# Attention scores on row-tiled halves of TensorE replaced by block-diagonal matmuls on the whole array

## The chip, the core and the metric

The kernel runs on one core of a Trainium2 chip. Its engines work in parallel, each through its own queue in order: TensorE (PE in the profile, with its weight loads as PEld), VectorE (DVE), ScalarE (ACT), GpSimd (POOL) and SyncE (SP, which here only issues DMAs). The metric is the device time of one execution in microseconds (us), the median of several runs.

## What is computed

Two stages. The first is attention within blocks whose keys and values are a soft permutation of blocks. For each of 4 batches and 8 heads, with 768 rows of 64 in 8 blocks of 96:

```
P = sort_net                                   # [4, 8, 8, 8]
5 times: P = exp(P - max); P /= row sums; P /= column sums
k_sorted = einsum('bhij,bhjcd->bhicd', P, k_b) # blocks of k mixed by P
v_sorted = einsum('bhij,bhjcd->bhicd', P, v_b)
scores   = q_b @ k_sorted^T / 8                # per block, 96 x 96
out      = softmax(scores) @ v_sorted
```

The second is a feed-forward network (FFN) on the 3072 x 512 result: `h = relu(x @ w_in)`, `out = (h * h) @ w_out`, with a hidden size of 2048.

## The kernel before

**Plan.** Every operation is put down with an engine, a cost and what it depends on; a list scheduler (`Plan.run`) works out an order, and the instructions are emitted in that order on every engine. For TensorE there are two queues, each in order: attention and FFN. An FFN "chunk" is the four up matmuls of one hidden tile or a quarter of one output tile's down matmuls; 28 chunks make a unit of 384 tokens, and there are 8 units. An attention stage's head goes ahead of the next FFN chunk once its due time, counted in chunks, is reached and its inputs are ready. `DUES` (lines 21 to 49) holds these due times by batch and stage: K (sort the second half of batch 0), S (scores), T (turn the values), A (scores times values), X (turn the result), V and N (sort values and keys in natural layout), Z (DMA transposes), Q (batch 1's first two pairs), L (loads). Attention stages are queued by due time, and stages whose due time is negative go as soon as they can. Batch 0's first half is in an order written out by hand (`FIRST`, line 53); FFN begins behind it at about 21.6 us.

**Tiles.** A `Unit` is a pair of heads (hp) of one batch. Both heads' q^T lie above each other on 128 partitions: head 0 on 0 to 63, head 1 on 64 to 127. Scores are computed in halves, that is in groups of four blocks (`s_sc`, line 641), into one of two PSUM slots (ring `r2`).

- The *row form* (line 665) is used for all of batch 0 and for the first two pairs of batch 1. Each block and head has a matmul of its own with 64 contraction rows and 96 columns: 8 per group, two of them on different row halves of the array at a time. The plan gives it 0.17 us and the mode "row"; each change of mode costs 0.1 us in the plan. Its q^T is in the `qT` tiles, written by `s_q` (line 523).
- The *wide form* (line 655) is used for the pairs from batch 1's third on (`u.tiled`). A buffer qz holds q^T block-diagonally, that is head 0 over zeros and zeros over head 1, side by side. One matmul with 128 contraction rows and 192 columns then does both heads of a block: 4 per group. The block-diagonal form is made by `q_split` (line 840): VectorE copies head 1's half to its place and zeroes where it was. GpSimd zeroes head 0's other half once (`make_zeros`, line 804), after batch 0, since the qz buffers are batch 0's value buffers (vs) until then.

ScalarE takes exp of a group (lines 685, 695, 701), TensorE multiplies by the values (line 871), VectorE normalises (lines 883 and 884), and the result is turned into xT, the FFN's input, by TensorE and a copy or by a DMA.

**Loads.** All inputs come by GpSimd DMAs, in order: batch 0, w_in, w_out, then batch 1's six loads (`loads_after`, line 379); later batches are loaded when the batch before them is done. xT (128 x 4 x 3072) is filled batch by batch; a region of it, that of the last batch, holds the selection matrix `sel` in the beginning (line 391).

Of the kernel before, what the change touches and what calls it, by code (L numbers as in the profile page):

```python
# [10 lines left out]
AF = mybir.ActivationFunctionType  # L11
# [9 lines left out]
DUES = {  # L21
    (0, "K"): (-130.0, -51.0, -121.0, -51.0),
    (0, "S"): (-63.0, -37.0, -72.5, -31.0),
    (0, "T"): (-110.5, -2.0, -40.5, -38.0),
    (0, "A"): (-47.0, 2.0, -9.5, -15.5),
    (0, "X"): (-8.5, 4.5, 11.0, -2.5),
    (0, "W"): (-102.5,),
    (1, "V"): (4.5, 5.0),
    (1, "Q"): (21.0,),
    (1, "N"): (None, 39.0),  # L30
    (1, "Z"): (None, None, 42.0, 44.5),
    (1, "S"): (26.0, 36.5, 43.0, 47.0),
    (1, "A"): (39.5, 41.0, 44.0, 48.5),
    (1, "X"): (41.0, 41.0, 49.0, 48.5),
    (2, "L"): (49.5,),
    (2, "N"): (57.0, 78.0),
    (2, "V"): (63.5, 89.0),
    (2, "Z"): (68.5, 90.0, 94.0, 91.0),
    (2, "S"): (90.5, 96.5, 99.5, 98.5),
    (2, "A"): (95.5, 96.5, 104.0, 103.5),  # L40
    (2, "X"): (96.5, 99.0, 118.5, 114.5),
    (3, "L"): (124.0,),
    (3, "N"): (138.5, 138.0),
    (3, "V"): (136.0, 143.0),
    (3, "Z"): (144.0, 146.5, 159.5, 156.0),
    (3, "S"): (151.5, 154.0, 160.0, 158.0),
    (3, "A"): (152.0, 156.0, 162.5, 158.0),
    (3, "X"): (162.0, 257.5, 169.0, 366.0),
}
# [135 lines left out]
def kernel(  # L185
# [10 lines left out]
    nc = tc.nc  # L196

    B, H, S, D = q.shape
# [5 lines left out]
    HP = H // 2  # L204
# [105 lines left out]
    w_out_bf = const.tile([128, NT, d_model], BF16)  # L310
    xT = const.tile([128, KC, n_tok], BF16)
    w_all = const.tile([128, H + HP, NB, C0], BF16)
    w_t = const.tile([128, NH // 4, 4, NB], BF16)
# [65 lines left out]
    def loads_after(deps):  # L379
        for g in range(4):  # L380
            if g == 1:
                landed["last"] = plan.add("DMA", 0.4, lambda e: None, [landed["last"]])
            t = slice(NT // 4 * g, NT // 4 * (g + 1))
            dma(("w_out", g), 1.05, lambda t=t: (w_out_bf[:, t, :], w_out_r[:, t, :]), deps)
        for t, g in ((2, 0), (2, 1), (1, 0), (0, 0), (1, 1), (0, 1)):
            load(1, t, HP * g, HP, deps=deps)

    rs = const.tile([NH, NB], FP32)
    cs = const.tile([NH, NB], FP32)
    pf = const.tile([NH, NB, NB], BF16)  # L390
    sel = xT[0:32, 0, 3 * S:3 * S + 32 * C0].rearrange("p (j c) -> p j c", c=C0)
    pt = const.tile([128, NB, NH], BF16)
# [112 lines left out]
    class Unit:  # L505


        def __init__(self, b, hp, halves):
            self.b, self.hp, self.halves = b, hp, halves
            self.tiled = in_tiles(b, 1, HP * (hp // 2))  # L510
            if self.tiled:
                self.i0, self.ni, self.full = 0, NB, True
                return
            self.n, self.old = rks.take()
            self.kvT = kvT_r[self.n]
            self.ksT, self.vsT = self.kvT[:, 0, :], self.kvT[:, 1, :]
            self.i0, self.ni = NQ * halves[0], NQ * len(halves)
            self.full = len(halves) == 2
# [4 lines left out]
    def s_q(b, hp, p0, p1, due=0, after=None, eng=AD):  # L523

        n = p1 - p0
        t = {}

        def mm(e):
            qb = qkv[b][0]
            if b == 0:  # L530
                t["p"] = psf.tile([128, NA, n], BF16, tag="pf", name="qtp")
            else:
                t["p"] = ps1.tile([128, NA, n], BF16, tag="p1", name="qtp")
            for a in range(NA):
                for h in range(2):
                    nc.tensor.transpose(
                        out=t["p"][64 * h:64 * (h + 1), a, :],
                        in_=qb[p0:p1, 2 * hp + h, D * a:D * (a + 1)],
                        identity=ident[p0:p1, p0:p1])
            if p0 == 0:  # L540
                tiles["qT", b, hp] = att.tile(
                    [128, NA, 128], BF16, tag="qT", name="qT", bufs=4)

        def ev(e):
            qT, src = tiles["qT", b, hp].rearrange("p a x -> p (a x)"), t["p"]
            if b == 0:
                copy(e, qT.rearrange("p (i c a) -> p i c a", a=NA, c=C0)
                     [:, p0 // C0:p1 // C0, :, :], src.rearrange("p a (i c) -> p i c a", c=C0))
            else:
                copy(e, qT.rearrange("p (i a c) -> p i a c", a=NA, c=C0)  # L550
                     [:, p0 // C0:p1 // C0, :, :], src.rearrange("p a (i c) -> p i a c", c=C0))

        if b == 0:
            dep = landed[b, 0, 0, p0]
        else:
            dep = landed[b, 0, HP * (2 * hp // HP), 0]
        ring = rf if b == 0 else r1
        s1, old = ring.take()
        if p0 == 0:
            qTs[b, hp], oldq = rqT.take()  # L560
        else:
            oldq = []
        pe = plan.add("PE", 0.04 + 0.0023 * n, mm, [dep, id_op] + old, due, mode="col")
        readers[b].append(pe)
        op = one_of(eng, cost_b(NA * n), ev, [pe, after] + oldq)
        ring.use(s1, pe, op)
        rqT.use(qTs[b, hp], op)
        return op
# [72 lines left out]
    def s_sc(u, due=0):  # L641
# [3 lines left out]
        for hf in u.halves:  # L645
# [4 lines left out]
            def mm(e, hf=hf, st=st, slot=slot):  # L650
                st["p"] = scp = p2[slot]
                if u.tiled:
                    for n in range(NQ):
                        i = NQ * hf + n
                        nc.tensor.matmul(  # L655
                            out=scp[:, n // 2, 2 * BLK * (n % 2):2 * BLK * (n % 2 + 1)],
                            lhsT=kx_r[u.kx][:, i::NB],
                            rhs=qz_r[u.qz][:, :, :, C0 * i:C0 * (i + 1)],
                            start=True, stop=True)
                    return  # L660
# [11 lines left out]
            u.et[hf], olde = ret.take()  # L672
            if u.tiled:
                pe = plan.add("PE", 0.33, mm, [u.k_op, u.q_op] + old, due)
                rkx.use(u.kx, pe)
                rqz.use(u.qz, pe)
            else:
# [5 lines left out]
            if u.b == 0:  # L683
                def ex(e, st=st, et=et_r[u.et[hf]]):
                    nc.scalar.activation(out=et[:, :, 0:HS], in_=st["p"][0:96, :, 0:HS],  # L685
                                         func=AF.Exp, scale=scale)

# [4 lines left out]
            for h in range(2):  # L692
                def ex(e, h=h, st=st, et=et_r[u.et[hf]]):
                    if u.tiled:
                        nc.scalar.activation(  # L695
# [4 lines left out]
                        return  # L700
                    nc.scalar.activation(
                        out=et[:, h, 0:HS].rearrange("p (n c a) -> p n c a", c=C0, a=NA),
                        in_=st["p"][0:96, h, 0:HS].rearrange("p (n a c) -> p n c a", c=C0, a=NA),
                        func=AF.Exp, scale=scale)
                op = plan.add("ACT", cost_f(HS)[0], ex, [pe] + olde)
# [98 lines left out]
    def make_zeros(e):  # L804
        for qz in qz_r:
            nc.gpsimd.memset(qz[0:64, 1, :, :], 0.0)

    def s_turn(b, hp):

# [29 lines left out]

        def q_split(e):  # L840
            nc.vector.tensor_copy(out=qz[64:128, 1, :, :], in_=qz[64:128, 0, :, :])
            nc.vector.memset(qz[64:128, 0, :, :], 0.0)

        sp = plan.add("SP", 1.4, q_turn, [qp, loaded(b)] + oldz + [op for ops in rvs.all for op in ops])
        q_op = plan.add("WAY", 1.3, lambda e: None, [sp])
        rqi.use(n, q_op)
        if not zeroed:
            last = [op for ops in rvs.all for op in ops if op.eng0 == "PE"]
            assert len(last) == 2 * HP
            zeroed.append(plan.add("POOL", 2.1, make_zeros, last))  # L850
        q_op = plan.add("DVE", 0.8, q_split, [q_op, zeroed[0]])
        rqz.use(z, q_op)
        return kx, z, k_op, q_op

    def s_av(u, due=0):
# [4 lines left out]
        for hf in u.halves:  # L860
# [4 lines left out]
            def mm(e, hf=hf, st=st, slot=slot):  # L865
# [3 lines left out]
                for n in range(NQ):  # L869
                    for h in range(2):  # L870
                        nc.tensor.matmul(  # L871
                            out=oup[:, h, 66 * n:66 * n + D + 1],
                            lhsT=(et_r[u.et[hf]].rearrange("p h x -> p (h x)")
                                  [:, BLK * (2 * n + h):BLK * (2 * n + h) + 128] if u.tiled else
                                  et_r[u.et[hf]][:, h, BLK * n:BLK * n + 128]),
# [187 lines left out]
    for hp in range(HP):  # L1063
        qops[hp] = s_q(0, hp, 0, 64, after=exps[2 + (hp + 2) // 3], eng="ACT")
    q2ops = [s_q(0, hp, 64, 128, after=exps[4], eng="ACT") for hp in range(HP)]
    op = plan.add("DVE", 0.25, p_turn, [step])
# [52 lines left out]
    def sort_second(b, n, due):  # L1119
        for hp in range(2):  # L1120
            units[1, hp] = Unit(1, hp, (0, 1))
            build_w(H + 2 * hp, 2, pt, x_done[0, 2, 1])
        units[1, 0].q_op = s_q(1, 0, 0, 128, due)
        for hp in range(2):
            units[1, hp].k_op = s_sort(units[1, hp], 1, due)
        units[1, 1].q_op = s_q(1, 1, 0, 128, due)

# [68 lines left out]
```

The softmax here doesn't subtract the row's maximum and nothing guards it: scores larger than these inputs give would overflow.

## Time and profile before

| | |
|---|---|
| time | 219.42 us, median of 3 (219.3 to 219.85) |
| span of the profiled execution | 218.0 us |
| PE busy | 211.4 us |
| FFN up matmuls (line 993) | 506 of 128 x 384 in the records, 88.4 us |
| FFN down matmuls (line 1023) | 353 of 128 x 512 in the records, 83.7 us |
| row-form scores (line 665) | 96 matmuls, 3.6 us |
| wide-form scores (line 655) | 80 matmuls, 9.2 us |

Busy times are the union of the modelled spans of an engine's instructions. Pipelined matmuls overlap in them, so where a matmul's price is wanted it is taken from the starts of successive groups. A timeline row of the profile reads: start in us, us from the first start to the last end, engine, line, operation, output <- inputs, shape, count, and in brackets how long the engine was idle before it and which event ended that. Some FFN down matmuls are missing from the records (353 of 368).

### The profile page before, as it was taken

How to read it: one execution, taken by the hardware profiler on the slowest of the kernel's cores; microseconds unless marked ns; L12 is line 12 of the kernel's file. 1: busy time of each engine (PE TensorE's matmuls, PEld its weight loads, DVE VectorE, ACT ScalarE, POOL GpSimd, SP SyncE). 2: the span in 40 equal slices, each digit the busy share in tenths (PEclk: the TensorE clock that was granted, in tenths of full speed). 3: DMA queues.
4: the chain of work that ended last, by engine and by line, in shares of the span. 5: the costliest groups of instructions: out<-in, count | busy, mean ns of one | idle time of the engine just before them, and what ended most of it. 6: DMA issues, size and time to landing. Idle time of an engine off the chain costs nothing.

```text
span 218.0 us, 4937 instructions
## 1 busy us (share of the span) xinstructions
PE 211.4 (97%) x1955; PEld 120.6 (55%) x1970; DVE 111.8 (51%) x313; ACT 119.3 (55%) x246; POOL 30.5 (14%) x55
## 2 busy tenths in 40 slices
PE   8989999999999999999999999999999999999994
PEld 3556666446566555445765465435666465456543
DVE  6778667347597437225786055066776155005300
ACT  4656796238944378227874276156865276137421
POOL 7986222200000510000000330000000000000000
PEclk9999999999999999999999999999999999999999
DMA  5999999999853499399872599569984310120012
GB/s 68 194 200 206 207 207 212 206 239 236 196 108 87 112 180 228 50 174 242 214 180 63 125 187 213 116 163 166 247 152 111 95 51 0 48 85 15 0 48 96
DMA packets 46583, 31.21 MB, mean 143 GB/s; under 512 B 26016, under 2 KB 41632, under 8 KB 46560
## 3 DMA queue, kind: packets, MB, share of 16 engines
q0 software_dynamic: 12736, 13.63, 38.1%
q1 hardware_dynamic: 33824, 17.27, 33.6%
q8 instruction: 15, 0.25, 0.4%
q14 instruction: 8, 0.07, 0.1%
HBM read 29.70 MB, written 8.72 MB: 176 GB/s over the span
## 4 chain that ended last, share of the span: by engine, by line
PE 87%; DMA 4%; POOL 3%; DVE 2%; issue 1%; ACT 1%; POOLq 0%; DVEq 0%; ACTq 0%
PE hp L993 36%; PE op L1023 36%; PE p L871 4%; DMA kb<-in_k_dram 4%; PE p L655 3%; PE p L757 2%; PE op L1051 2%; PE p L665 1%; POOL kb L322 1%; POOL vb L322 1%; PE xtp L924 1%; ACT h L1001 1%; PE p L622 1%; DVE h L1004 1%; PE vbp L721 1%
## 5 line engine op out<-in xcount | busy, mean ns | idle before, releaser
L993 PE MATMUL hp<-xT,w_in_bf 128*128 128x384 bf16 x506 | 88.4, 326 | 0.1
L1023 PE MATMUL op<-w_out_bf,h 128*128 128x512 bf16 x353 | 83.7, 379 | 0.9 <-issue 0.2
L1004 DVE TENSOR_TENSOR h<-h 128x384 bf16<-128x384 bf16 x128 | 44.6, 356 | 55.3 <-ACT h L1001 54.4
L1001 ACT ACTIVATE h<-hp 128x384 bf16<-128x384 f32 x128 | 61.7, 494 | 18.4 <-PE hp L993 14.4
L993 PEld LDWEIGHTS <-w_in_bf 128*128 128x128 bf16 x506 | 47.6, 98 | 31.1 <-issue 1.1
L1023 PEld LDWEIGHTS <-h 128*128 128x128 bf16 x368 | 34.3, 98 | 36.9 <-issue 0.9
L248 ACT COPY ob<-op 128x512 f32<-128x512 f32 (+2 forms) x24 | 13.6, 567 | 52.9 <-PE op L1023 50.4
L884 DVE TENSOR_TENSOR ao<-p,rec 96x512 bf16<-96x512 f32 x32 | 22.0, 686 | 1.1
L695 ACT ACTIVATE et<-p 96x384 bf16<-96x384 f32 x40 | 16.8, 489 | 9.2 <-PE p L655 8.9
L871 PEld LDWEIGHTS <-et 96*128 96x128 bf16 x256 | 11.5, 97 | 4.5 <-issue 0.7
L1135 POOL COPY held<-xT 1x3 bf16<-1x3 bf16 (+1 forms) x2 | 0.4, 183 | 78.4 <-DMA xT<-ao 78.4
L883 DVE RECIPROCAL rec<-p 96x8 f32<-96x8 f32 x32 | 6.4, 200 | 8.4 <-PE p L871 8.0
L416 PE MATMUL p<-ones 128*128 128x512 bf16 (+1 forms) x30 | 9.4, 434 | 1.1 <-DVE ones L269 1.1
L250 DVE CAST vn<-p 128x768 bf16<-128x768 f32 x6 | 5.7, 958 | 9.1 <-PE p L757 8.9
L655 PEld LDWEIGHTS <-kx 128*128 128x128 bf16 x80 | 8.5, 144 | 2.4 <-issue 0.5
L871 PE MATMUL p<-vblk,et 96*128 96x65 bf16 x192 | 9.5, 193 | 0.0
L655 PE MATMUL p<-qz,kx 128*128 128x192 bf16 x80 | 9.2, 246 | 0.0
L250 DVE CAST kn<-p 128x768 bf16<-128x768 f32 x5 | 4.8, 958 | 6.4 <-PE p L757 6.4
L322 POOL DMA_DIRECT2D kb<-in_k_dram x10 | 6.4, 642 | 4.4 <-DMA w_in_bf<-in_moe_w_in_dram 2.0
L322 POOL DMA_DIRECT2D vb<-in_v_dram x10 | 6.3, 629 | 3.6 <-DMA w_in_bf<-in_moe_w_in_dram 3.6
L322 POOL DMA_DIRECT2D qb<-in_q_dram x8 | 6.1, 768 | 4.6 <-DMA w_out_bf<-in_moe_w_out_dram 2.1
L685 ACT ACTIVATE et<-p 96x768 bf16<-96x768 f32 x8 | 6.1, 803 | 0.0
(85 smaller groups left out, 126.9 us busy)
## 6 DMA issues: line engine op xcount, KB each, us to landing
out_dram<-ob SPq DMA_DIRECT2D x23, 256.0 KB, 2.0
qb<-in_q_dram POOLq DMA_DIRECT2D x8, 384.0 KB, 11.5
v_way<-vn SPq DMA_DIRECT2D x6, 396.0 KB, 5.1
vblk<-v_way SPq DMA_DIRECT2D x6, 396.0 KB, 4.1
vb<-in_v_dram POOLq DMA_DIRECT2D x6, 384.0 KB, 12.0
kb<-in_k_dram POOLq DMA_DIRECT2D x6, 384.0 KB, 10.6
w_in_bf<-in_moe_w_in_dram POOLq DMA_DIRECT2D x4, 512.0 KB, 12.2
w_out_bf<-in_moe_w_out_dram POOLq DMA_DIRECT2D x4, 512.0 KB, 17.2
```

The source lines that it names most:

```text
L248: nc.scalar.copy(out=out, in_=in_)
L250: nc.vector.tensor_copy(out=out, in_=in_)
L322: nc.gpsimd.dma_start(out=dst, in_=src)
L416: nc.tensor.matmul(out=p2[slot][:, 0, 0:128 * r].rearrange("p (r x) -> p r x", r=r), lhsT=ones, rhs=ones[:, None, :].to_broadcast([128, r, ...
L655: nc.tensor.matmul(out=scp[:, n // 2, 2 * BLK * (n % 2):2 * BLK * (n % 2 + 1)], lhsT=kx_r[u.kx][:, i::NB], rhs=qz_r[u.qz][:, :, :, C0 * i: ...
L695: nc.scalar.activation(out=et.rearrange("p h x -> p (h x)")[:, HS * h:HS * (h + 1)] .rearrange("p (m c a) -> p m c a", c=C0, a=NA), in_=st ...
L871: nc.tensor.matmul(out=oup[:, h, 66 * n:66 * n + D + 1], lhsT=(et_r[u.et[hf]].rearrange("p h x -> p (h x)") [:, BLK * (2 * n + h):BLK * (2 ...
L884: nc.vector.tensor_tensor(out=u.ao[:, n0:n0 + NQ, :, :].rearrange("p n e d -> p e n d"), in0=ov[:, :, :, 0:D], in1=rec[:, :, :, None].to_b ...
L993: nc.tensor.matmul(out=t["hp", nt][:, 0:HS], lhsT=w_in_bf[:, kc, 128 * nt:128 * (nt + 1)], rhs=xT[:, kc, t0:t0 + HS], start=(kc == 0), sto ...
L1001: nc.scalar.activation(out=t["h1", nt], in_=t["hp", nt][:, 0:HS], func=AF.Relu)
L1004: nc.vector.tensor_tensor(out=t["h2"][:, nt, :], in0=t["h1", nt], in1=t["h1", nt], op=ALU.mult)
L1023: nc.tensor.matmul(out=t["op", mt], lhsT=t["h2"][:, nt, 128 * mt:128 * (mt + 1)], rhs=w_out_bf[:, nt, :], start=(nt == 0), stop=(nt == NT ...
```

## The change

The row form stays only for batch 0's first half, which is under way before the FFN. Two more sets of units get the wide form (`self.wide = b > 0 or halves == (1,)`): batch 0's second half and batch 1's first two pairs. Eight groups of scores are concerned. For this

- batch 0's second-half q^T is evicted into xT's region of the last batch, which is free till then (`q0_r`: 128 x 2 x 384 for each pair). VectorE zeroes head 0's other half at the very start; GpSimd copies head 1's half over and zeroes where it was, for each pair, behind the issue of the w_out loads. Batch 1's loads are issued after these splits. `sel` moves to batch 2's region.
- batch 1's first two q^T are evicted into qz buffers and split there by VectorE, as the later ones are. They now take turns in the ring of three qz buffers, and have to wait for batch 0's values and for `make_zeros`.
- the exps write, and the matmuls with the values read, the layout of the wide form.
- all due times are new.

The aim is to have these score groups run without a change of TensorE's tiling mode. The core of the diff (the due times that the prediction speaks of, then the code):

```diff
 DUES = {
-    (0, "K"): (-130.0, -51.0, -121.0, -51.0),
-    (0, "S"): (-63.0, -37.0, -72.5, -31.0),
+    (0, "K"): (-155.0, -32.0, -154.0, -54.0),
+    (0, "S"): (-44.5, -15.0, -54.0, -21.0),
...
-    (1, "V"): (4.5, 5.0),
-    (1, "Q"): (21.0,),
-    (1, "N"): (None, 39.0),
-    (1, "Z"): (None, None, 42.0, 44.5),
-    (1, "S"): (26.0, 36.5, 43.0, 47.0),
-    (1, "A"): (39.5, 41.0, 44.0, 48.5),
-    (1, "X"): (41.0, 41.0, 49.0, 48.5),
+    (1, "V"): (1.5, 15.5),
+    (1, "Q"): (9.0,),
+    (1, "N"): (None, 21.5),
+    (1, "Z"): (None, None, 24.0, 25.0),
+    (1, "S"): (17.0, 23.0, 35.5, 38.5),
+    (1, "A"): (30.0, 26.5, 37.5, 45.5),
+    (1, "X"): (32.0, 28.5, 44.5, 45.5),
...
+    q0_r = [xT[:, hp, n_tok - S:n_tok].rearrange("p (h x) -> p h x", h=2) for hp in range(HP)]
+    for hp in range(HP):
+        nc.vector.memset(q0_r[hp][0:64, 1, :], 0.0)
...
+        for hp in range(HP):
+            def split(e, hp=hp):
+                nc.gpsimd.tensor_copy(out=q0_r[hp][64:128, 1, :], in_=q0_r[hp][64:128, 0, :])
+                nc.gpsimd.memset(q0_r[hp][64:128, 0, :], 0.0)
+
+            q2ops[hp] = plan.add("POOL", 1.1, split, [q2ops[hp], landed["w_out", 3].deps[0]])
         for t, g in ((2, 0), (2, 1), (1, 0), (0, 0), (1, 1), (0, 1)):
-            load(1, t, HP * g, HP, deps=deps)
+            load(1, t, HP * g, HP, deps=[q2ops[HP - 1]])
...
-    sel = xT[0:32, 0, 3 * S:3 * S + 32 * C0].rearrange("p (j c) -> p j c", c=C0)
+    sel = xT[0:32, 0, 2 * S:2 * S + 32 * C0].rearrange("p (j c) -> p j c", c=C0)
...
+            self.wide = b > 0 or halves == (1,)
...
-                if u.tiled:
+                if u.wide:
                     for n in range(NQ):
                         i = NQ * hf + n
                         nc.tensor.matmul(
                             out=scp[:, n // 2, 2 * BLK * (n % 2):2 * BLK * (n % 2 + 1)],
-                            lhsT=kx_r[u.kx][:, i::NB],
-                            rhs=qz_r[u.qz][:, :, :, C0 * i:C0 * (i + 1)],
+                            lhsT=(kx_r[u.kx][:, i::NB] if u.tiled else
+                                  u.ksT[:, BLK * i:BLK * i + 128]),
+                            rhs=(qz_r[u.qz][:, :, :, C0 * i:C0 * (i + 1)] if u.b > 0 else
+                                 q0_r[u.hp][:, :, BLK * n:BLK * (n + 1)]),
                             start=True, stop=True)
...
+    def split_q(z, op):
+
+        def q_split(e):
+            qz = qz_r[z]
+            nc.vector.tensor_copy(out=qz[64:128, 1, :, :], in_=qz[64:128, 0, :, :])
+            nc.vector.memset(qz[64:128, 0, :, :], 0.0)
+
+        if not zeroed:
+            last = [op for ops in rvs.all for op in ops if op.eng0 == "PE"]
+            assert len(last) == 2 * HP
+            zeroed.append(plan.add("POOL", 2.1, make_zeros, last))
+        return plan.add("DVE", 0.8, q_split, [op, zeroed[0]])
...
-        units[1, 0].q_op = s_q(1, 0, 0, 128, due)
+        units[1, 0].qz, units[1, 0].q_op = s_q(1, 0, 0, 128, due)
```

More of the change, by code (lines that the diff above doesn't have):

```diff
@@ L21 @@
 DUES = {
-    (0, "K"): (-130.0, -51.0, -121.0, -51.0),
-    (0, "S"): (-63.0, -37.0, -72.5, -31.0),
[L24 to L27, printed above, removed]
-    (1, "V"): (4.5, 5.0),
-    (1, "Q"): (21.0,),
-    (1, "N"): (None, 39.0),
-    (1, "Z"): (None, None, 42.0, 44.5),
-    (1, "S"): (26.0, 36.5, 43.0, 47.0),
-    (1, "A"): (39.5, 41.0, 44.0, 48.5),
-    (1, "X"): (41.0, 41.0, 49.0, 48.5),
[L35 to L48, printed above, removed]
+    (0, "K"): (-155.0, -32.0, -154.0, -54.0),
+    (0, "S"): (-44.5, -15.0, -54.0, -21.0),
+    (0, "T"): (-116.5, -15.0, -40.5, -45.5),
+    (0, "A"): (-40.0, -5.5, 4.0, -11.5),
+    (0, "X"): (-32.5, 8.5, 8.5, -1.0),
+    (0, "W"): (-102.0,),
+    (1, "V"): (1.5, 15.5),
[5 more added lines that the diff above has]
+    (1, "X"): (32.0, 28.5, 44.5, 45.5),
+    (2, "L"): (62.5,),
+    (2, "N"): (68.5, 80.0),
+    (2, "V"): (67.5, 88.5),
+    (2, "Z"): (70.0, 86.0, 88.5, 98.0),
+    (2, "S"): (91.0, 97.0, 97.5, 101.5),
+    (2, "A"): (96.5, 98.0, 102.0, 104.0),
+    (2, "X"): (103.0, 131.5, 124.5, 120.5),
+    (3, "L"): (135.0,),
+    (3, "N"): (140.0, 141.5),
+    (3, "V"): (136.5, 141.0),
+    (3, "Z"): (140.5, 144.5, 152.5, 145.0),
+    (3, "S"): (148.0, 150.0, 157.5, 155.5),
+    (3, "A"): (148.5, 153.5, 157.5, 155.5),
+    (3, "X"): (157.0, 229.0, 175.0, 311.5),
 }
@@ L539, in mm @@
                         identity=ident[p0:p1, p0:p1])
-            if p0 == 0:
+            if b == 0 and p0 == 0:
                 tiles["qT", b, hp] = att.tile(
@@ L544, in ev @@
         def ev(e):
[L545 to L551, printed above, removed]
+            src = t["p"]
+            if b > 0:
+                copy(e, qz_r[z][:, 0, :, :], src)
+                return
+            if p0 > 0:
+                copy(e, q0_r[hp][:, 0, :].rearrange("p (i c a) -> p i c a", a=NA, c=C0),
+                     src.rearrange("p a (i c) -> p i c a", c=C0))
+                return
+            qT = tiles["qT", b, hp].rearrange("p a x -> p (a x)")
+            copy(e, qT.rearrange("p (i c a) -> p i c a", a=NA, c=C0)
+                 [:, p0 // C0:p1 // C0, :, :], src.rearrange("p a (i c) -> p i c a", c=C0))
         if b == 0:
@@ L558, in s_q @@
         s1, old = ring.take()
-        if p0 == 0:
+        oldq = []
+        if b > 0:
+            z, oldq = rqz.take()
+            oldq = oldq + [op for ops in rvs.all for op in ops]
+        elif p0 == 0:
             qTs[b, hp], oldq = rqT.take()
-        else:
-            oldq = []
         pe = plan.add("PE", 0.04 + 0.0023 * n, mm, [dep, id_op] + old, due, mode="col")
@@ L566, in s_q @@
         ring.use(s1, pe, op)
-        rqT.use(qTs[b, hp], op)
+        if b > 0:
+            rqz.use(z, op)
+            op = split_q(z, op)
+            rqz.use(z, op)
+            return z, op
+        if p0 == 0:
+            rqT.use(qTs[b, hp], op)
         return op
@@ L672, in s_sc @@
             u.et[hf], olde = ret.take()
-            if u.tiled:
+            if u.wide:
                 pe = plan.add("PE", 0.33, mm, [u.k_op, u.q_op] + old, due)
-                rkx.use(u.kx, pe)
-                rqz.use(u.qz, pe)
+                if u.tiled:
+                    rkx.use(u.kx, pe)
+                else:
+                    rks.use(u.n, pe)
+                if u.b > 0:
+                    rqz.use(u.qz, pe)
             else:
@@ L684, in ex @@
                 def ex(e, st=st, et=et_r[u.et[hf]]):
-                    nc.scalar.activation(out=et[:, :, 0:HS], in_=st["p"][0:96, :, 0:HS],
-                                         func=AF.Exp, scale=scale)
+                    nc.scalar.activation(
+                        out=(et.rearrange("p h x -> p (h x)")[:, 0:2 * HS]
+                             .rearrange("p (h x) -> p h x", h=2) if u.wide else et[:, :, 0:HS]),
+                        in_=st["p"][0:96, :, 0:HS], func=AF.Exp, scale=scale)
                 op = plan.add("ACT", cost_f(2 * HS)[0], ex, [pe] + olde)
@@ L693, in ex @@
                 def ex(e, h=h, st=st, et=et_r[u.et[hf]]):
-                    if u.tiled:
+                    if u.wide:
                         nc.scalar.activation(
@@ L700, in ex @@
                         return
[L701 to L704, printed above, removed]
                 op = plan.add("ACT", cost_f(HS)[0], ex, [pe] + olde)
@@ L838, in q_turn @@
                 out=qz[:, 0, :, :], in_=qi_r[n].rearrange("p a e d -> p (a e d)"))
-        def q_split(e):
-            nc.vector.tensor_copy(out=qz[64:128, 1, :, :], in_=qz[64:128, 0, :, :])
-            nc.vector.memset(qz[64:128, 0, :, :], 0.0)
         sp = plan.add("SP", 1.4, q_turn, [qp, loaded(b)] + oldz + [op for ops in rvs.all for op in ops])
@@ L846, in s_turn @@
         rqi.use(n, q_op)
[L847 to L851, printed above, removed]
+        q_op = split_q(z, q_op)
         rqz.use(z, q_op)
@@ L873, in mm @@
                             lhsT=(et_r[u.et[hf]].rearrange("p h x -> p (h x)")
-                                  [:, BLK * (2 * n + h):BLK * (2 * n + h) + 128] if u.tiled else
+                                  [:, BLK * (2 * n + h):BLK * (2 * n + h) + 128] if u.wide else
                                   et_r[u.et[hf]][:, h, BLK * n:BLK * n + 128]),
@@ L1064 @@
         qops[hp] = s_q(0, hp, 0, 64, after=exps[2 + (hp + 2) // 3], eng="ACT")
-    q2ops = [s_q(0, hp, 64, 128, after=exps[4], eng="ACT") for hp in range(HP)]
+    q2ops = {hp: s_q(0, hp, 64, 128, after=exps[4], eng="ACT") for hp in range(HP)}
     op = plan.add("DVE", 0.25, p_turn, [step])
@@ L1122, in sort_second @@
             build_w(H + 2 * hp, 2, pt, x_done[0, 2, 1])
-        units[1, 0].q_op = s_q(1, 0, 0, 128, due)
+        units[1, 0].qz, units[1, 0].q_op = s_q(1, 0, 0, 128, due)
         for hp in range(2):
             units[1, hp].k_op = s_sort(units[1, hp], 1, due)
-        units[1, 1].q_op = s_q(1, 1, 0, 128, due)
+        units[1, 1].qz, units[1, 1].q_op = s_q(1, 1, 0, 128, due)
     def turn(b, hp, due):
```

## The prediction

> **What bounds the kernel now.** I read the page's busy times and slices first, then the chain, then TensorE's timeline, window by window.
>
> ```profile
> PE 211.4 (97%) x1955; PEld 120.6 (55%) x1970; DVE 111.8 (51%) x313; ACT 119.3 (55%) x246; POOL 30.5 (14%) x55
> ...
> PE   8989999999999999999999999999999999999994
> ...
> PEclk9999999999999999999999999999999999999999
> ...
> PE 87%; DMA 4%; POOL 3%; DVE 2%; issue 1%; ACT 1%; POOLq 0%; DVEq 0%; ACTq 0%
> ```
>
> TensorE is busy in every slice at full clock and makes up 87% of the chain that ended last; VectorE and ScalarE are at half load. A busy PE need not be a PE at its peak, so I took starts, not durations. A long run of FFN up matmuls (64 from 124.59 to 134.99 us) gives 10.40/64 = 0.1625 us each; down matmuls, by starts, give 0.216. With these prices the time from the end of the start-up (21.6 us) to the end has little air: the attention groups in between are filled by FFN work. So the question is how much TensorE time the change adds or removes, and whether PE waits anywhere.
>
> **The old form of the scores**, in the timeline of PE:
>
> ```profile
> 50.56 0.53 PE L536 MATMUL qtp<-ident,qb 128*64 128x128 bf16 x12
> 51.02 0.51 PE L665 MATMUL p<-qT,kvT 64*128 64x96 bf16 x16
> 51.47 2.12 PE L993 MATMUL hp<-xT,w_in_bf 128*128 128x384 bf16 x12
> 53.52 0.35 PE L665 MATMUL p<-qT,kvT 64*128 64x96 bf16 x8
> 53.80 2.77 PE L993 MATMUL hp<-xT,w_in_bf 128*128 128x384 bf16 x16
> 56.51 0.34 PE L665 MATMUL p<-qT,kvT 64*128 64x96 bf16 x8
> ```
>
> One group (8 matmuls, half of a head pair's blocks) holds PE from 53.52 to 53.80, 0.28 us; two in a row from 51.02 to 51.47, 0.45 us. The difference, 0.17 us, is the streaming of a group, and 0.11 us is paid once on leaving. Entering costs as much: the 16 up matmuls from 53.80 should take 2.60 us and the next group starts after 2.71.
>
> **The new form** exists already in later batches:
>
> ```profile
> 102.17 1.48 PE L993 MATMUL hp<-xT,w_in_bf 128*128 128x384 bf16 x8
> 103.48 0.82 PE L655 MATMUL p<-qz,kx 128*128 128x192 bf16 x8
> 104.14 2.11 PE L993 MATMUL hp<-xT,w_in_bf 128*128 128x384 bf16 x12
> ...
> 116.81 0.74 PE L871 MATMUL p<-vblk,et 96*128 96x65 bf16 x16
> 117.61 0.81 PE L1023 MATMUL op<-w_out_bf,h 128*128 128x512 bf16 x3
> ```
>
> Two groups of four take 103.48 to 104.14, 0.33 us each, and the 8 up matmuls before them take 1.31 for 1.30: no price for entering. So a lone group is 0.28 + 0.11 = 0.39 us in row form and 0.33 in wide form, but a pair is 0.45 + 0.11 = 0.56 against 0.66, and a pair beside other tiled work, which has to switch anyway, is cheaper still. Wide wins only alone.
>
> **What the Trainium skill says.** TensorEngine Tiling (Array Packing), Key Properties: changing the tiling mode drains TensorE. The trace agrees; its price is the 0.11 us above. TensorE: Matmul & The Clock Gate, Back-to-back issue gap: a warm matmul takes N/2.4 + 2.5 ns, which is 82.5 ns at N = 192; the trace has 0.33/4 = 0.0825 us. The same page, Part 3: row tiles run concurrently; 96 columns are then 42.5 ns per pair and 0.17 us per four pairs, the trace's number. SBUF — State Buffer, on the shared port pair: GpSimd and a VectorE instruction in a two-port mode, or with two SBUF inputs against a GpSimd read, block each other. Before shows no stretching: GpSimd builds w_all at 14.26 to 16.10 us, and the VectorE eviction at 14.37 takes 0.42 us, as it does at 31.46 without GpSimd.
>
> **The change part by part.**
>
> *Scores.* Eight groups change: four of batch 0's second half, two for each of batch 1's first two pairs. Before they stand in five places: pairs at 25.86, 31.35 and 51.02, single ones at 53.52 and 56.51. Streaming was 8 x 0.17 = 1.36 us and becomes 8 x 0.33 = 2.64. Switches saved: three places stand between full-array work (2 x 0.11 each); the pairs at 25.86 and 51.02 follow column-tiled work that must switch back anyway, one each. That is 8 x 0.11 = 0.88. Net +0.40 us on PE.
>
> *Due times.* Before, the sorts of pairs 1 and 3 have the same due (-51) and run together at 27.71. Now they are at -32 and -54 with five other stages between, so column mode is entered and left once more: +0.2 us. The other tiled stages remain about as separate as they were.
>
> *Start-up.* Four memsets of 64 x 384 bf16 come ahead of the normalisation on VectorE:
>
> ```profile
> 1.95 0.21 DVE L305 MEMSET et<- 96x32 uint32 x4
> 2.66 0.21 DVE L398 TENSOR_REDUCE rs<-p_sb 32x8 f32<-32x64 f32 x1 [0.50 <-ACT p_sb L430]
> ```
>
> The kx memsets (128 uint32) take 0.15 us each, the split's (384 uint32) 0.38, so one of 192 is about 0.21 and four 0.85. VectorE is free at 2.16, so the first reduction moves from 2.66 to about 3.0: +0.35 on the chain that ends in w_all at 12.1. PE then waits on loads anyway (0.30 us at 15.94 for vb, 0.22 at 16.90 for kb), so most is swallowed there; VectorE's backlog from 15.4 us lets about 0.1 through. Bounds 0 and 0.35; I take 0.1.
>
> *GpSimd's splits.* Four times a copy and a memset of 64 x 384:
>
> ```profile
> 16.05 3.03 POOL L322 DMA_DIRECT2D w_out_bf<-in_moe_w_out_dram  x4
> 20.63 0.55 POOL L322 DMA_DIRECT2D vb<-in_v_dram  x1 [1.55 <-DMA w_in_bf<-in_moe_w_in_dram]
> 23.22 0.54 POOL L322 DMA_DIRECT2D vb<-in_v_dram  x1 [2.04 <-DMA w_in_bf<-in_moe_w_in_dram]
> ...
> 34.24 0.73 POOL L806 MEMSET qz<- 64x768 bf16 x1
> 39.00 1.41 POOL L806 MEMSET qz<- 64x768 bf16 x2 [4.02 <-PE p L871]
> ```
>
> 768 columns of memset take 0.73, so 384 about 0.4. No such copy is in the trace: at least 0.4 as the memset, at most 0.65, as the two-input builds of 256 columns (0.64). A split is 0.8 to 1.1 us, four end at 22.3 to 23.5. The six loads queued behind them would have gone at 20.63 and 23.22: the first is up to 2.9 us late, the second under 1, and from the third (25.74) on they wait, as now, for earlier transfers to land. At 23.5 us two transfers of w_in and four of w_out, 512 KB each, are still to land, so the DMA engines don't run dry: zero. The first score of the second half ran at 25.86: the splits are done.
>
> *VectorE's splits of batch 1.* Two of 0.36 + 0.38 us, both shown at L841 and L842, and the zeroing by GpSimd ahead of them (after batch 0's last A at 38.5 in before, and done by 40.4, while q of batch 1 is first transposed at 48.68). They lengthen the way from q to scores by 0.8 us; FFN chunks fill PE in the meantime, and VectorE's queued squares have half an engine to spare: zero. The exps keep count and size.
>
> *Sum:* +0.40 + 0.2 + 0.1 = +0.7 us, 219.4 -> 220.1, if PE's waits stay as they are.
>
> **What the waits could give or take.** By starts, PE loses about 2.0 us to waits after 21.6 us, in some ten places: the two value groups above take 117.61 - 116.81 = 0.80 against 0.50 elsewhere; two score groups
>
> ```profile
> 69.76 0.88 PE L655 MATMUL p<-qz,kx 128*128 128x192 bf16 x8
> 70.69 0.81 PE L1023 MATMUL op<-w_out_bf,h 128*128 128x512 bf16 x3
> ```
>
> take 0.93 against 0.66. The new due times reshuffle all of these.
>
> **Rivals.** (1) *The new order loses less*: without pairs to keep together, scores spread, batch 1 is done some chunks earlier (dues 28.5 to 45.5 for its last stage against 41 to 49), its successor's loads start earlier, and 1.3 to 1.7 of the 2.0 us vanish. 220.1 - 1.5 = 218.6. For it: all dues are new. Against: waits are scattered and small, each with its own cause. (2) *A new wait*: batch 1's second V (due 15.5) now stands behind Q (due 9), which can't run before its data land at about 48; before, it ran at 44.64. Its way through memory (issue to landing 5.1 + 4.1 us) then starts some 6 us later, SyncE's queue holds stores and transposes behind it, and the third pair's transposed q waits for the first pair's scores, as its buffer is now shared. With one or two waits of 0.5 to 1 us, or the whole 0.35 at the start: 221.4. Against: FFN has 28 chunks in which to hide this. (3) *They cancel*: 219.5, the waits shrink by just what PE gains.
>
> **Numbers.** Forecast 0.45, at 220.1; it spreads upwards, since the start can cost 0.35 and a new order has more ways to wait, so three parts in ten of it lie within 0.3% (219.42 +- 0.66). Rival 1 0.33, rival 2 0.12, rival 3 0.1. Faster 0.33; same 0.1 + 0.13 = 0.23; slower 0.32 + 0.12 = 0.44. Range 218.2 to 221.4: it takes in most of rival 1, all of 3, the bounds of the start (0 to 0.35), and half of rival 2.
>
> **What would show it.** Right: L665 falls from 96 to 32 matmuls, the wide groups take 0.33 us from start to start, the first reduction starts at about 3.0, the loads from kb on are issued as before, PE's total after 21.6 us grows by 0.6. Wrong: FFN runs with hardly any excess over 0.1625 and 0.216 per matmul and its switches (rival 1), or an idle PE of over 0.5 us between 40 and 76 us (rival 2).

## The result, and the profile after

The changed kernel takes **220.81 us** (median of 4 runs, 220.69 to 221.42), beside 219.51 us for the kernel before on the same chip: a ratio of 1.0063, with a 95% interval from 1.0040 to 1.0086. It is slower, by 1.3 us.

The page of the changed kernel, its busy times, slices and chain:

```profile
PE 212.8 (97%) x1923; PEld 122.2 (56%) x1938; DVE 111.8 (51%) x318; ACT 120.5 (55%) x249; POOL 33.9 (15%) x63
...
PE   8989999999999999999999999999999999999994
...
PE 87%; DVE 6%; DMA 2%; ACT 2%; issue 1%; SPq 0%; DVEq 0%
```

Nothing has taken TensorE's place: it fills 87% of the chain as before. Its busy time rose by 1.4 us with 32 fewer recorded instructions. GpSimd gained 3.4 us, by the four splits of batch 0, and has left the chain. So the answer lies in TensorE's own queue.

**An account of TensorE.** For both kernels I took TensorE's timeline from the first sort of batch 0's second half (22.2 us before, 22.05 after) to the end, always from start to next start of a run of equal matmuls, as the prediction did. Each run is charged its streaming (count times 0.1625 us for an up matmul, 0.216 down, 0.0825 wide score, 0.17 a row group, and so on). Where the next run is in another tiling mode, up to 0.11 us of the excess is a mode change. The rest is waiting. Counts come from the program's order where records are missing. The streaming column also holds the 3.0 us from the last matmul to the end of the execution, the same in every kernel here.

| TensorE, us | streaming | mode changes | waits | sum |
|---|---|---|---|---|
| before | 190.5 | 3.96 (40 of them) | 1.4 | 195.8 |
| changed | 191.7 | 3.11 (32) | 2.2 | 197.0 |
| difference | +1.28 | -0.85 | +0.8 | +1.2 |

These are sums of one profiled execution each, and the 1.2 us agree with the 1.3 us of the medians. They have a place too: up to the end of the up matmuls of the second token unit (63.42 us before, 64.46 after) the changed kernel's TensorE needs 1.21 us more, and from there to the end both need 154.6 us. So the whole difference, new waits included, arises in the first third of the execution.

The stretch in which batch 1 is scored, TensorE's timeline of the changed kernel (columns: start, busy us, engine, line, operation, output and inputs, count):

```profile
50.51 0.53 PE L546 MATMUL qtp<-ident,qb 128*64 128x128 bf16 x12
50.97 0.47 PE L783 MATMUL p<-vb,w_t 32*32 32x384 bf16 x16
51.37 1.48 PE L1024 MATMUL hp<-xT,w_in_bf 128*128 128x384 bf16 x8
52.68 0.82 PE L677 MATMUL p<-qz,kvT 128*128 128x192 bf16 x8
53.34 1.46 PE L1024 MATMUL hp<-xT,w_in_bf 128*128 128x384 bf16 x8
54.74 0.62 PE L783 MATMUL p<-kb,w_t 32*32 32x384 bf16 x16
55.29 1.47 PE L1024 MATMUL hp<-xT,w_in_bf 128*128 128x384 bf16 x8
56.60 0.82 PE L677 MATMUL p<-qz,kvT 128*128 128x192 bf16 x8
57.26 2.79 PE L1024 MATMUL hp<-xT,w_in_bf 128*128 128x384 bf16 x16
60.21 0.66 PE L902 MATMUL p<-vblk,et 96*128 96x65 bf16 x16 [0.17 <-DMA vblk<-v_way]
```

Read the starts. The eight up matmuls from 51.37 take 1.31 us to the wide scores at 52.68: 8 x 0.1625, entering costs nothing. Two wide groups take 0.66 (52.68 to 53.34), 0.33 each. The values of batch 1's second group (V, L783 on vb) now stand right behind the transposes of q, both in tiled modes. The keys (N, L783 on kb) hold TensorE for 0.55 us (54.74 to 55.29), where a sort of this size needs 0.21 and a mode change 0.11: a wait of 0.23. The 16 up matmuls from 57.26 take 2.95 for 2.60: a wait of 0.35 for `vblk` (sorted values of batch 1, which SyncE's DMAs write to memory and read back). These two and smaller ones at 42.7 and 51 us are the new waits in this part.

What happened to the splits on GpSimd:

```profile
18.48 0.50 POOL L390 COPY xT<-xT 64x384 bf16<-64x384 bf16 x1
19.04 0.41 POOL L391 MEMSET xT<- 64x384 bf16 x1
...
22.16 1.09 POOL L325 DMA_DIRECT2D vb<-in_v_dram  x2
25.01 0.75 POOL L325 DMA_DIRECT2D kb<-in_k_dram  x1 [1.76 <-DMA w_in_bf<-in_moe_w_in_dram]
```

Each split is 0.50 + 0.41 = 0.91 us, the last of four ends at 22.2, and the loads go on at 22.16, the third already waiting for an earlier transfer, as in the kernel before.

### The profile page after: what moved, and what is told of

It reads as the page before. It is cut to its first block, busy times and chain, and to the rows that moved or that the text cites. A ratio compares the mean times of both kernels' runs of the same rounds, so it can differ in the third digit from the quotient of the medians.

```text
span 219.1 us, 4877 instructions
## 1 busy us (share of the span) xinstructions
PE 212.8 (97%) x1923; PEld 122.2 (56%) x1938; DVE 111.8 (51%) x318; ACT 120.5 (55%) x249; POOL 33.9 (15%) x63
## 4 chain that ended last, share of the span: by engine, by line
PE 87%; DVE 6%; DMA 2%; ACT 2%; issue 1%; SPq 0%; DVEq 0%
PE op L1054 36%; PE hp L1024 35%; PE p L677 4%; PE p L902 4%; DMA vblk<-v_way 2%; PE p L783 2%; PE op L1082 2%; PE vbp L747 1%; DVE p_sb L409 1%; PE xtp L955 1%; PE p L644 1%; ACT h L1032 1%; ACT et L725 1%; DVE cs L407 1%; DVE ao L915 1%
## 5 line engine op out<-in xcount | busy, mean ns | idle before, releaser
L1035 DVE TENSOR_TENSOR h<-h 128x384 bf16<-128x384 bf16 x128 | 44.0, 356 | 49.6 <-ACT h L1032 48.9
L248 ACT COPY ob<-op 128x512 f32<-128x512 f32 (+2 forms) x25 | 14.2, 568 | 57.7 <-PE op L1054 55.2
L725 ACT ACTIVATE et<-p 96x384 bf16<-96x384 f32 x48 | 20.1, 491 | 6.2 <-PE p L677 5.7
L425 PE MATMUL p<-ones 128*128 128x512 bf16 (+1 forms) x30 | 10.3, 470 | 1.1 <-DVE ones L269 1.1
```

The costliest lines, as they stand in the source:

```text
L248: nc.scalar.copy(out=out, in_=in_)
L425: nc.tensor.matmul(out=p2[slot][:, 0, 0:128 * r].rearrange("p (r x) -> p r x", r=r), lhsT=ones, rhs=ones[:, None, :].to_broadcast([128, r, ...
L725: nc.scalar.activation(out=et.rearrange("p h x -> p (h x)")[:, HS * h:HS * (h + 1)] .rearrange("p (m c a) -> p m c a", c=C0, a=NA), in_=st ...
L1035: nc.vector.tensor_tensor(out=t["h2"][:, nt, :], in0=t["h1", nt], in1=t["h1", nt], op=ALU.mult)
```

## The experiments

The theory: TensorE pays for the form of the scores (streaming up, mode changes down), the new due times add waits, and the splits and memsets lie off the path. The rivals: the due times alone are to blame; or the start-up chain behind VectorE's memsets; or the second V behind Q; or GpSimd's splits ahead of its loads. The expectations below put numbers on each.

**e1_old_dues: the form, with the old due times**

```
 DUES = { ... }     # all entries as in the kernel before
```

> The changed code with the due times of before: the wide form stays, the order goes back (34 changes of mode behind the start-up instead of 40 in before and 32 in the changed kernel). Theory (the price of the form and the waits of the new order, about half each): streaming +1.28 us against before, six switches less -0.65, waits as in before, start 0 to +0.2: 220.2 us, that is about +0.3% over before. Rival 'all waits' (the form costs nothing, the new order costs 1.3): 219.5. Rival 'all form' (the wide form and its splits cost 1.3, the order nothing): 220.8.

Measured: 221.02 us, ratio 1.0066 (1.0042 to 1.0090). So the due times alone aren't to blame; but it is also slower than I expected of the form. The due times aren't the order: the scheduler also reads the costs of the stages (0.33 for a wide group against 0.17, the splits), and gave an order that is not that of the kernel before. TensorE's sums are 191.7 streaming, 3.31 mode changes, 2.2 waits, one of them of 0.57 us at 112.8, in batch 2. So e1 doesn't isolate the form; e8 below does it properly.

**e2_new_dues: the old form, with the new due times**

```
 DUES = { ... }     # all entries as in the changed kernel, code as before
```

> The code of before, row form, with the new due times. Its order has 46 changes of mode, six more than before. Theory: +0.65 us for the switches and +0.7 to 0.9 for the waits of the new order: 220.9 us, as slow as the changed kernel. Rival 'all waits': 220.8 too, but with the waits alone making up 1.3. Rival 'all form': 219.5, as before.

Measured: 220.60 us, 1.0041 (1.0025 to 1.0058). The new due times are slower with the old form as well: 46 mode changes (4.61 us) and 2.25 us of waits against 3.96 and 1.4. They don't explain it alone, since here they cost 0.65 us in mode changes, which the changed kernel doesn't have.

**e3_zero_gpsimd: the four memsets at the start moved off VectorE**

```
-    for hp in range(HP):
-        nc.vector.memset(q0_r[hp][0:64, 1, :], 0.0)
...
             def split(e, hp=hp):
...
+                nc.gpsimd.memset(q0_r[hp][0:64, 1, :], 0.0)
```

> The changed kernel with the four memsets of q0 on GpSimd, in the splits, instead of on VectorE ahead of the normalisation. Theory: the first reduction starts 0.3 us earlier, w_all 0.2 earlier, little of it reaches the end: 220.7 us (0 to -0.2); GpSimd's 1.6 us more are free, as the loads behind them wait for earlier transfers from the third on. Rival 'the start is on the path': 220.5 or less (-0.35). Rival 'GpSimd is on the path': slower by 0.5 to 1.6.

Measured: 220.91 us, 1.0061 (1.0038 to 1.0083), no gain against 220.81. The first reduction is 0.25 us late in the changed kernel (2.91 against 2.66) and w_all 0.2. In e3 both are earlier again, by 0.18 us each, and the first sort of the second half stands at 21.88 instead of 22.05. But this is lost again at the wait for `vblk`: the 16 up matmuls ahead of it take 3.15 us (57.08 to 60.23) instead of 2.95. So the rival's 0.35 us isn't there; an effect of 0.1 is too small for these intervals.

**e4_v1_first: the second V before Q**

```
-    (1, "V"): (1.5, 15.5),
+    (1, "V"): (1.5, 5.0),
```

> The changed kernel with one due time put back: batch 1's second V at 5.0, ahead of Q, instead of 15.5, behind it. V then writes to memory some 6 us earlier, and the read of the first V's values isn't held up in SyncE's queue. Theory: the wait of 0.36 us ahead of batch 1's first values (57 to 60 us) and part of the one behind N go, one switch comes back: 220.4 us (-0.4). Rival 'all form': no change, 220.8 to 220.9. Rival 'all waits, by V behind Q': 219.5 to 219.8.

Measured: 221.49 us, 1.0083 (1.0060 to 1.0106): slower still. The `vblk` wait goes (16 up matmuls take 2.60 us, 57.41 to 60.01), but another stands there:

```profile
55.49 1.46 PE L1024 MATMUL hp<-xT,w_in_bf 128*128 128x384 bf16 x8
57.41 2.76 PE L1024 MATMUL hp<-xT,w_in_bf 128*128 128x384 bf16 x16 [0.46 <-ACT h L1032]
```

Eight up matmuls should take 1.30 us and the next start comes after 1.92: 0.62 us in which TensorE waits for ScalarE's relu. So putting V ahead doesn't mend the order: one wait went, a longer one came. But e4 doesn't clear V behind Q, which the prediction's rival 2 named, of the `vblk` wait. SyncE now issues the read 0.73 us earlier than in the changed kernel (55.28):

```profile
54.55 0.56 SPq L813 DMA_DIRECT2D vblk<-v_way  x1
```

In e2, on the other hand, V stands behind Q as well, and the 12 up matmuls ahead of these values take 1.96 us for 1.95, so V behind Q alone doesn't make the wait. Keys and FFN matmuls moved along with V in e4, so its own waits can't be put down to V alone.

**e5_wide_twice: the wide scores of the eight groups streamed twice**

```
-                    for n in range(NQ):
+                    for n in [n for n in range(NQ) for _ in range(1 if u.tiled else 2)]:
```

> The changed kernel, with each matmul of the eight score groups that the change made wide issued twice (the same result written again); the plan isn't told, so the order stays. It prices the new form on the path. Theory (PE bounds, 0.33 us of streaming a group, nothing hides it): +2.6 us over the changed kernel, 223.4 us. Rival 'hidden' (the scores lie beside waits that they can fill, so that the form costs the path nothing): 220.8 to 221.5.

Measured: 223.31 us, 1.0173 (1.0153 to 1.0192): +2.5 us against the changed kernel. TensorE's streaming grew by 2.65 (194.35), the 8 x 0.33 of the prediction. Not all of the 2.65 was paid at once: the doubled matmuls filled the two waits shown above (the 16 up matmuls now take 2.60 us, 59.65 to 62.25), and up to the end of the second token unit's up matmuls TensorE needs only 2.06 us more than in the changed kernel. In the profiled execution a late read of `vblk` then adds a wait of 0.76 us, so the 2.5 us can hold some of that too. TensorE's time passes through to the end, less the waits that it fills.

**e6_row_twice: the old row groups streamed twice**

```
-                for n in range(NQ):
+                for n in [n for _ in range(1 if u.b == 0 and hf == 0 else 2) for n in range(NQ)]:
```

> The kernel before, with each row-form group of batch 0's second half and of batch 1 issued twice in a row, without another change of mode. It prices the old form. Theory: 8 x 0.17 = +1.4 us, 220.8 us. Rival (two row tiles don't really stream side by side, so that a group costs as much as a wide one, 0.33): +2.6, 222.1. The difference between this and the doubled wide form is the streaming that the change adds: theory 1.3 us.

Measured: 221.10 us, 1.0071 (1.0056 to 1.0086): +1.6 us on the kernel before, of which TensorE's sum shows 1.36 = 8 x 0.17. Together with e5 this prices the swap directly, each by TensorE's sum: 2.64 - 1.36 = 1.28 us, the difference of streaming in the table.

**e7_copy_thrice: GpSimd's copy three times in each split**

```
-                nc.gpsimd.tensor_copy(out=q0_r[hp][64:128, 1, :], in_=q0_r[hp][64:128, 0, :])
+                for _ in range(3):
+                    nc.gpsimd.tensor_copy(out=q0_r[hp][64:128, 1, :], in_=q0_r[hp][64:128, 0, :])
```

> The changed kernel with the copy in each of GpSimd's splits issued three times (the same data again): four microseconds more on GpSimd, ahead of batch 1's loads. Theory: GpSimd is off the path, its loads wait for earlier transfers anyway and the splits are done before their scores: 220.8 us, no change. Rival 'GpSimd is on the path' (through the loads or the splits): 221.5 to 224.

Measured: 220.99 us, 1.0067 (1.0052 to 1.0083), within the changed kernel's interval. The same queue of GpSimd:

```profile
18.48 1.64 POOL L391 COPY xT<-xT 64x384 bf16<-64x384 bf16 x3
...
26.96 1.09 POOL L325 DMA_DIRECT2D vb<-in_v_dram  x2
```

The loads go 4.8 us later than in the changed kernel and the end doesn't move: the splits ahead of the loads aren't the cause.

**e8_form_only and e9_order_only: each half of the change with the other's order.** After e1 and e2 I gave the scheduler the costs that belong to the order wanted, so that e8 has the new form in the old kernel's order, and e9 the old form in the changed kernel's.

```
 # e8: changed code, DUES of before, and
-                pe = plan.add("PE", 0.33, mm, [u.k_op, u.q_op] + old, due)
+                pe = (plan.add("PE", 0.33, mm, [u.k_op, u.q_op] + old, due) if u.tiled else
+                      plan.add("PE", 0.17, mm, [u.k_op, u.q_op] + old, due, mode="row"))
 # e9: code of before, DUES of the changed kernel, and
-                pe = plan.add("PE", 0.17, mm, [u.k_op, u.q_op] + old, due, mode="row")
+                pe = (plan.add("PE", 0.33, mm, [u.k_op, u.q_op] + old, due)
+                      if u.b > 0 or u.halves == (1,) else
+                      plan.add("PE", 0.17, mm, [u.k_op, u.q_op] + old, due, mode="row"))
```

> The form alone: the changed code with the due times of before, and the plan told the old cost (0.17, mode row) for the eight groups, so that TensorE's order is exactly that of before, with wide groups in the places of the row ones. Theory (form and order each cost about half): streaming +1.28, eight switches less -0.86, waits as in before: +0.4 us, 219.9. Rival 'all form': 220.8. Rival 'all order': 219.5.

> The order alone: the code of before, row form, with the new due times and the plan told the new cost (0.33, no change of mode) for the eight groups, so that TensorE's order is exactly that of the changed kernel, with row groups in the places of the wide ones. Theory: two switches more than before +0.2, the waits of the new order +0.6: 220.2 us. Rival 'all form': 219.5. Rival 'all order': 220.8.

| | streaming | mode changes | waits | sum | median us | ratio (95%) |
|---|---|---|---|---|---|---|
| before | 190.5 | 3.96 | 1.4 | 195.8 | 219.46 | 1 |
| e8, form only | 191.7 | 3.11 (32) | 1.4 | 196.2 | 220.08 | 1.0028 (1.0017 to 1.0039) |
| e9, order only | 190.5 | 4.18 (42) | 3.2 | 197.8 | 220.72 | 1.0059 (1.0036 to 1.0083) |
| changed | 191.7 | 3.11 (32) | 2.2 | 197.0 | 220.81 | 1.0063 (1.0040 to 1.0086) |

This is the run that decides. The form alone costs +0.43 us on TensorE and leaves the waits where they were; +0.62 us in the medians, with an interval from 0.37 to 0.86. TensorE's timeline of e8, the same places that the prediction showed of before at 51.02, 53.52 and 56.51:

```profile
51.29 0.83 PE L677 MATMUL p<-qz,kvT 128*128 128x192 bf16 x8
51.96 2.11 PE L1025 MATMUL hp<-xT,w_in_bf 128*128 128x384 bf16 x12
53.91 0.49 PE L677 MATMUL p<-qz,kvT 128*128 128x192 bf16 x4
54.24 2.76 PE L1025 MATMUL hp<-xT,w_in_bf 128*128 128x384 bf16 x16
```

The pair takes 0.67 us (0.45 before), the single group 0.33 (0.28 before), and the 12 up matmuls in between 1.95 = 12 x 0.1625 exactly, without the 0.11 that ahead of a row group they used to lose. So the gain per place is there; the pair gives it back.

The order costs the rest. In e9's profiled execution 1.07 us of the 3.2 us of waits are one wait, in TensorE's timeline, for a DMA:

```profile
164.23 0.49 PE L655 MATMUL p<-qz,kx 128*128 128x192 bf16 x4
165.63 0.41 PE L873 MATMUL p<-vblk,et 96*128 96x65 bf16 x8 [0.91 <-ACT et L697]
```

and the same execution's DMA view from 158 to 166 us, with the time from issue to landing last:

```profile
vblk<-v_way SPq DMA_DIRECT2D x1, 396.0 KB, 6.2
```

In the kernel before the same read takes 4.5 us, in the changed one 4.4. The exponentials (ACT et) of these scores were done at 164.43, and the read landed at 165.50, 0.13 us ahead of the matmuls; in e5 and e12 too they follow the landing by 0.14. It was the read. Without it e9 has 2.1 us of waits, as the changed kernel has. So the order adds 0.7 to 0.8 us of waits with either form, by single profiled executions. The medians don't add up: 0.62 for the form and 1.26 for the order are 1.88 us, beside 1.30 for both. e9's executions spread from 220.13 to 222.77 us, and in how many of them the read is late isn't known; the fastest is 0.67 above the median of before. That the order costs time is shown by e9, its size only roughly.

**e10_read_first: the read of `vblk` of batch 1's first group ahead of the q transpose.** In the changed kernel SyncE issues a transpose of q first and the read behind it:

```profile
53.91 1.31 SPq L876 DMA_TRANSPOSE qz<-qi  x1
55.28 0.56 SPq L813 DMA_DIRECT2D vblk<-v_way  x1
```

In the kernel before, the read was issued at 53.83.

```
-        there = plan.add("WAY", 9.7 if b == 1 and g == 0 else 3.2, lambda e: None, [wr], tail=0.8)
+        there = plan.add("WAY", 8.0 if b == 1 and g == 0 else 3.2, lambda e: None, [wr], tail=0.8)
...
-        back = plan.add("WAY", 3.5, lambda e: None, [rd], tail=0.7)
+        back = plan.add("WAY", 5.0 if b == 1 and g == 0 else 3.5, lambda e: None, [rd], tail=0.7)
```

> The changed kernel with two numbers of the plan for batch 1's first values altered: their way to memory 8.0 instead of 9.7, their way back 5.0 instead of 3.5. The read then stands ahead of the transposes in SyncE's queue and the values are used two FFN chunks later. Theory: the wait of 0.36 us ahead of these values (57 to 60 us) goes and nothing comes back there: 220.4 us (-0.4). Rival (a wait taken away at one place comes back at the next, as every new order brings its own): 220.7 to 221.2.

Measured: 225.94 us, 1.0273 (1.0238 to 1.0309). The read is now issued at 53.02, ahead of the transposes, and the wait for `vblk` is gone (24 up matmuls from 57.25 to the values at 61.17 take 3.92 us for 3.90), but the values also stand eight up matmuls later, and the scheduler, given two other costs, also moved batch 3's scores to later, and the last units of the FFN waited for their input. Its waits of PE:

```profile
PE hp L1024 <- DMA xT<-ao: 3.6, 1, 3.6
```

By starts TensorE loses 5.4 us there (173.5 us). The run agrees with the late issue of the read as a cause of that wait, without isolating it. The issue isn't all of it: from issue to landing this read takes 4.9 us in the changed kernel (5.1 in e3, 5.0 in e7), but 4.0 in the kernel before and 4.2 in e9, which issues it at 55.40 in the same order and waits only 0.14 us. e10 also shows that a changed cost moves more of the order than the place it was meant for.

**e11_row_spread and e12_one_sort: the kernel before, with three due times moved or one.** Two waits of the kernel before are in batch 3: one of 0.27 us behind N (145.42) and one of 0.24 behind S.

```
 # e11, on the kernel before
-    (3, "N"): (138.5, 138.0),
+    (3, "N"): (140.5, 138.0),
...
-    (3, "S"): (151.5, 154.0, 160.0, 158.0),
-    (3, "A"): (152.0, 156.0, 162.5, 158.0),
+    (3, "S"): (153.0, 154.0, 160.0, 158.0),
+    (3, "A"): (154.5, 156.0, 162.5, 158.0),
 # e12: the N line alone
```

> The kernel before, row form and its order up to batch 3, with three due times of batch 3 altered so that its two key sorts and its first scores stand further apart (waits of 0.27 and 0.24 us in before). Theory (these two waits go, nothing comes back): 218.9 to 219.1 us, faster than both kernels. Rival (every new order brings its own waits): 219.4 to 220.2.

> The kernel before, row form, with one due time of batch 3 altered (the first pairs' key sort at 140.5 instead of 138.5), so that four more FFN matmuls stand between the two key sorts and nothing else in TensorE's order moves. Theory: the wait of 0.27 us behind the second sort goes, and no other comes, since the order is otherwise the same: 219.2 us, about -0.1% (at the edge of what is measured), the wait's going being seen in the timeline. Rival (the wait comes back elsewhere): 219.5 to 219.8.

Measured: e11 219.85 us, 1.0007 (0.9993 to 1.0020), no difference; its N wait is gone, the S wait stays and a new one of 0.61 us comes at 172.7. e12 **219.20 us, 0.9979 (0.9967 to 0.9991)**: the fastest of all that ran, ahead of both kernels, though only by 0.1 to 0.3% of the kernel before (219.68 us in this comparison). TensorE's timeline of e12:

```profile
143.79 0.38 PE L757 MATMUL p<-kb,w_t 32*32 32x384 bf16 x16
144.11 1.90 PE L1023 MATMUL op<-w_out_bf,h 128*128 128x512 bf16 x8
145.94 0.38 PE L757 MATMUL p<-kb,w_t 32*32 32x384 bf16 x16
```

The two halves of N, with eight down matmuls between them, leave after 0.32 and 0.31 us; nothing waits. So a wait of this kind is a matter of spacing two sorts. The wait that went was 0.27 us, the medians differ by 0.48 (0.2 to 0.7): a single due time is worth about as much as the whole form of the scores (0.43 us). The profiled execution of e12, itself 220.35 us, has a wait of 1.18 us for `vblk`; the medians are the better measure of it.

## Why the prediction was right, and where it wasn't

**Bound and price list: right.** TensorE's time passes through to the end (e6, and e5 but for the waits that it fills), and starts give prices that add up: 0.33 us a wide group, 0.17 a row group, 0.11 a mode change.

**Scores, +0.40: right.** e8 shows +0.43 on TensorE: +1.28 streaming, -0.85 for eight mode changes. Wide scores win only alone, as the working had it. What the Trainium skill's TensorEngine Tiling (Array Packing), Key Properties, says, that changing the mode drains TensorE, has its price here: 3.96 us for 40 changes and 3.11 for 32 are 0.10 us each, in row, column and 32x32 modes alike.

**Due times, +0.2: wrong.** Splitting the sorts of pairs 1 and 3 costs only one change more, as pair 3's sort stands right behind W (25.54 and 25.70), and the second V, which now follows the q transposes directly (50.51 to 50.97 above), saves one. The changed kernel has 32 changes, exactly as e8 with the old order. With row groups the new order would have had the two more that I put down (e9: 42 beside 40), but there the wide form saves ten and not eight. I had checked one pair of stages and called the others "about as separate as they were".

**Start-up, +0.1: not seen, nearer the bound 0.** The reduction came at 2.91 as foretold (about 3.0), but the first sort of the second half stands at 22.05, ahead of 22.22 in the kernel before, and at 21.87 in e12, which has the start-up of before: the delay is smaller than this spread. e3, without the memsets on VectorE, was no faster.

**GpSimd's splits, zero: right.** 0.91 us each, within the 0.8 to 1.1; e7 adds 4.8 us in front of the loads for nothing. What the Trainium skill's SBUF — State Buffer, Who interferes with whom, says, that a VectorE instruction with two SBUF inputs contends with a GpSimd one that reads SBUF, is to be seen in e7, where VectorE's squares of the FFN run beside GpSimd's copies. First VectorE and GpSimd of e7, then VectorE of the changed kernel, whose GpSimd is done with the splits by then:

```profile
24.98 1.19 DVE L1036 TENSOR_TENSOR h<-h 128x384 bf16<-128x384 bf16 x2
...
24.66 1.88 POOL L391 COPY xT<-xT 64x384 bf16<-64x384 bf16 x3
...
24.88 0.35 DVE L1035 TENSOR_TENSOR h<-h 128x384 bf16<-128x384 bf16 x1
25.52 0.36 DVE L1035 TENSOR_TENSOR h<-h 128x384 bf16<-128x384 bf16 x1 [0.29 <-ACT h L1032]
```

Two squares take 1.19 us instead of 0.71 (two in a row at 23.92 of the changed kernel), three copies 1.88 instead of 1.64; nothing of it reaches the end. The instruction in which the prediction saw no stretching, an eviction, is no such case: its one input is in PSUM. **VectorE's splits of batch 1, zero**: also hidden, since e8 has them and no more waits than before.

**"If PE's waits stay as they are": the step that failed.** It stood in the sum at zero and is worth +0.8 us, nearly two thirds of the result. The errors on the other steps (-0.2, -0.1) cancelled part of it, and so 220.1 ended only 0.7 us short, in part by luck: the +0.4 alone would have ended 1.0 short. The form alone doesn't bring it (e8: 1.4 as before), the new order does (e9, e2). Rival 2 had the mechanism, new waits of under a microsecond, and with V behind Q and SyncE's queue it named a possible part of one of them, `vblk`; that is 0.35 of the 0.8, and e4, which puts V ahead, is slower as a whole. Its sign, an idle PE of over 0.5 us between 40 and 76 us, didn't come: the longest wait there is the 0.35. The waits that came are small and scattered: `vblk`, read late by SyncE and slow to land (0.35; e4 and e10 agree), N on its PSUM slot, which by the trace the exponentials of the scores at 52.68 still held (0.23; a wait of the same size at N of batch 3 went with the spacing in e12), 0.47 at 155.9, others of 0.1. The one at 155.9 takes the place of the two in batch 3 that the kernel before had; those ahead of 64.46 us are the 0.8. Rival 1, fewer waits, wasn't seen; no profiled execution with the new due times had less than 2.2 us.

**The 2.0 us of waits that I read in the kernel before were 1.4.** A part of it isn't waiting at all. The two places at 69.76 and 116.81 that I counted as waits are followed by "x3" where four down matmuls run: the record of the first is missing, and the run ahead of it seems longer by one matmul's 0.216 us (353 of 368 down matmuls have a record). It made rival 1's stake larger than it was.

**What stays open.** Why the new order has just these waits, and why the first read of `vblk` takes 4.9 us in it, isn't settled; of the edits to the changed kernel, e4 and e10 each took the wait for `vblk` away and made a longer one elsewhere. Whether the new form would pay in an order planned for it wasn't tried.

## What to carry to other kernels

Price a change of form on the bounding engine in full: streaming plus mode changes, place by place; a row-tiled pair of 8 matmuls each already shares its switches, so a wide form with double streaming wins only where a group stands alone. Don't put an unknown reordering at zero: in a kernel that waits for only 1.4 of 196 us, a new order has more to lose than to win, and here it lost 0.8. And before a gap counts as a wait, look whether it is a multiple of one matmul and the block behind it is one short.

## What the runs showed of the hardware

The same read of 396 KB (`vblk` of batch 3, issued by SyncE at 159 to 161 us) takes 4.4 to 4.5 us from issue to landing in the profiled executions of the kernel before, of the changed kernel and of e8, but 5.3 in e12, 6.2 in e9 and 6.5 in e5, and TensorE then waits 0.75 to 1.2 us. That is as much as the changes that were measured, so one profiled execution says little of a wait for a DMA; what lengthens the read wasn't settled. Executions of the same kernel spread by some of it, 220.13 to 222.77 us for e9. I had also not expected that GpSimd's copy of 64 x 384 bf16 takes 0.50 us, only 0.09 more than a memset of that size.
